# Two attention problems on one core: a longer list of fixed-point heads, four P buffers, earlier terms at a unit's end, a warmed TensorE and a shorter tail

## Chip, cores, metric

The kernel runs on one core of a Trainium2 chip. The metric is device time in microseconds, a median over runs.

## The reference

Two attention blocks read different inputs of 2048 rows, 512 columns, 32 heads of 16, and write side by side.

```python
# A: causal attention inside 4 segments of 512 rows, plus a memory of the earlier segments
for s in range(4):
    p = softmax(qs @ ks.T * 0.25 + causal_mask)
    o = g * (phi(qs) @ M) / (phi(qs) @ z + 1e-6) + (1 - g) * (p @ vs)
    M, z = M + phi(ks).T @ vs, z + phi(ks).sum()
# B: full softmax attention over 2048 keys
o = softmax(q @ k.T * 0.25) @ v
out = concat([oA @ A_wo, oB @ B_wo])
```

B dominates: 32 heads x 2048 queries x 2048 keys of exponentials.

## The kernel before

The kernel cuts the work into *units*: 512 queries and four heads, 32 units of A and 32 of B. A B unit has 64 *banks* of scores (16 key blocks x 4 heads, each 128x512 in one PSUM bank). Two engines make the exponential. ScalarE takes tiles of three or two banks, writes bf16 into a P buffer. VectorE makes it in fixed point: it adds a constant to the scaled score, stores int16 into a pD buffer, and reads the bits as f16; two further copies, offset by constants ("terms"), are each multiplied by its own scaled copy of V, and the three sum to a good exponential. So a bank on VectorE costs an *eviction* from PSUM, two cheap additions, and three value matmuls instead of one.

The order of all instructions is decided when the program is built: a Python loop keeps a clock for each engine and issues what its rules allow. TensorE executes in that order.

```python
PDB, PTB, XB = 3, 3, 5                     # pD, P and input buffers
E1 = [(13, 0), (14, 1), (15, 2)]           # second heads for VectorE: (key block, head)
u["dl"] = [(kb, kb % 4, kb) for kb in range(NSB)] + [(kb, j, NSB + n) for n, (kb, j) in enumerate(E1)]
                                           # 16 + 3 = 19 banks of a B unit meant for VectorE
def pick(u, n, but=None):                  # the banks of ScalarE's next tile
    if not nbanks(u):                      # ScalarE's own are gone: it takes VectorE's leftovers
        ...
def dve_adds():                            # the two further terms of a finished pair of banks
    ...
# [cut] in the loop:
if (pd_open["add"] is not None or pd_open["tile"] is not None) and du is None and c["dve"] + 300 <= t:
    dve_close(); continue                  # terms of an open pair: when VectorE has been idle
if (rd and (even >= 3 or done or ...) and (act_soon is None or act_soon > t + 200)):
    flush(u, 16 if done else min(even, 4) if even >= 3 else 3); continue    # value matmuls
```

```python
def setup_gates():                         # emitted before the first scores
    nc.scalar.activation(gcol[:], beta_t[:], ACT.Exp, scale=-1.0)   # waits for beta's DMA
    # [cut] VectorE: gcol, omg, mqg; GpSimd: maskg
    init_v(VP_b, NSB)                      # GpSimd memsets
    for m in mbds:
        nc.gpsimd.memset(m[:], 0.0)
```

The tail runs twelve output matmuls ahead of the last unit's last value matmuls, then that unit's finish, four output matmuls, four casts, and a check of the range of all 1024 columns of row sums, whose result (a flag) decides whether a slow general path must run.

## Time and profile before

| | before |
|---|---|
| median | 974.75 us |
| span of the profiled run | 976.6 us |
| busy: ScalarE, VectorE | 864.9, 753.5 us |
| evictions by VectorE / banks of B by ScalarE | 534 / 1514 |
| first exponential | 17.01 us |
| ScalarE's gaps from the first to the last exponential | 79.3 us |
| end of the last exponential to the end | 19.76 us |

The last three rows are counted from the timeline. An engine's busy time is a union; its gaps are what is left of a stretch.

From the page: the span, the busy times, and three groups. A group line holds line, engine, operation, output and input, shapes and count, then total busy us, mean ns of one, then idle us ahead of them and who ended it.

```profile
span 976.6 us, 18041 instructions
...
PE 822.3 (84%) x6974; PEld 255.7 (26%) x6974; DVE 753.5 (77%) x1502; ACT 864.9 (89%) x803; POOL 373.0 (38%) x768
...
L734 ACT ACTIVATE pT<-s_ps 128x1536 bf16<-128x1536 f32 (+2 forms) x613 | 701.5, 1253 | 68.8 <-PE d_ps L775 38.0
L786 DVE TENSOR_SCALAR pD<-d_ps 128x512 int16<-128x512 f32 x534 | 350.1, 680 | 56.6 <-PE d_ps L775 54.4
...
L752 DVE TENSOR_SCALAR pD<-pD 128x1024 int16<-128x1024 int16 (+1 forms) x538 | 234.1, 477 | 0.3
...
```

A bank costs ScalarE 701.5/1514 = 0.463 us and VectorE (350.1 + 234.1)/534 = 1.09 us. ScalarE is nearest to full.

What ended ScalarE's waits from 100 to 950 us (us in total, times, longest us):

```profile
...
ACT pT L734 <- PE d_ps L775: 38.0, 48, 3.3
ACT pT L734 <- PE s_ps L729: 23.4, 30, 6.8
...
```

The first line reads: ScalarE's next scores stood in TensorE's order behind a score matmul for VectorE (d_ps).

The start on the timeline (start, duration, engine and line, operation; in brackets the idle time before and what ended it), first ScalarE:

```profile
...
17.01 2.15 ACT L677 ACTIVATE pT<-s_ps 128x1280 bf16<-128x1280 f32 x2 [0.49 <-PE s_ps L667]
21.50 2.15 ACT L677 ACTIVATE pT<-s_ps 128x1280 bf16<-128x1280 f32 x2 [2.35 <-PE s_ps L667]
...
26.78 2.15 ACT L677 ACTIVATE pT<-s_ps 128x1024 bf16<-128x1024 f32 x2 [2.63 <-PE s_ps L667]
```

and GpSimd:

```profile
...
19.32 0.21 POOL L167 TENSOR_TENSOR maskg<-jm,mq 128x16 f32<-128x16 f32 x1 [15.26 <-issue]
...
21.66 1.44 POOL L134 MEMSET VP_b<- 128x64 bf16 x16
...
23.27 1.84 POOL L173 MEMSET mbd<- 128x1024 bf16 x2
25.07 3.22 POOL L688 TENSOR_SCALAR_AFFINE_SELECT pT<-pT 128x384 bf16<-128x384 bf16 x7
```

and TensorE:

```profile
...
17.89 3.25 PE L327 MATMUL d_ps<-wv_a,xT_a 128*128 128x512 bf16 x8
...
25.65 0.76 PE L877 MATMUL acc<-pT,VP_a 128*32 128x512 bf16 x5 [2.58 <-POOL pT L688]
...
```

GpSimd's gate masks and memsets ran from 19.3 to 25.1 us. The causal masks of the first units (L688) waited for them, TensorE's value matmuls waited 2.58 us for a mask, and the scores behind them came late: ScalarE stood idle for 2.63 us. Its 2.35 us of idle time before that had another cause: eight matmuls of a V projection (L327) stood ahead of the scores in TensorE's order until 21.1 us.

The tail on the timeline:

```profile
...
956.44 2.75 PE L494 MATMUL s_ps<-wo_b,OT 128*128 128x512 bf16 x12 [0.54 <-ACT pT L734]
...
964.67 0.67 DVE L1088 TENSOR_SCALAR g<-RA 128x1024 f32<-128x1024 f32 x1
...
966.05 1.23 DVE L1092 TENSOR_TENSOR g<-g,g 128x1024 f32<-128x1024 f32 x1
...
967.31 1.22 DVE L1101 TENSOR_REDUCE okc<-g 128x1 f32<-128x1024 f32 x1
...
969.47 0.15 DVE L1105 CAST flag<-okc 128x1 int32<-128x1 f32 x1 [0.55 <-POOL okc L1104]
```

The range check is the three middle lines shown, 964.67 to 968.53 us, with one more cut; the line at 969.47 us writes the flag.

### The profile page before, as it was taken

What the parts mean: (1) busy time and instruction counts of PE and PEld (TensorE: products, weight loads), DVE (VectorE), ACT (ScalarE), POOL (GpSimd) and SP (SyncE); (2) the same over time, 40 slices, a digit from 0 to 9 for tenths busy, and PEclk for the clock granted to TensorE, in tenths of its full rate; (3) what the DMA queues carried; (4) which work ended last, traced back from release to release, by engine and by line L of the source; (5) the groups of instructions that cost most, each with busy time, mean ns of one, the idle gap of its engine ahead of it and who ended that gap; (6) DMA issues with size and microseconds to landing.
All of it is one profiled execution on the core that took longest, in us unless ns stands there. A gap on an engine that the chain in (4) does not pass through costs nothing.

```text
span 976.6 us, 18041 instructions
## 1 busy us (share of the span) xinstructions
PE 822.3 (84%) x6974; PEld 255.7 (26%) x6974; DVE 753.5 (77%) x1502; ACT 864.9 (89%) x803; POOL 373.0 (38%) x768
## 2 busy tenths in 40 slices
PE   5999998888888888898888898788988878888784
PEld 2333232222222222232222222222322222222221
DVE  3454668787888788869888987987478987989774
ACT  3898979898998889899999998989999998989982
POOL 3850625233333443444443154326345421514320
PEclk9999999898998999899999999999989998989977
DMA  7011000000000000010000000000000000000001
GB/s 221 23 44 39 6 22 2 1 1 2 1 2 12 12 1 1 6 34 1 1 1 18 6 1 1 1 1 3 22 1 12 12 1 2 1 1 1 1 7 42
DMA packets 14719, 13.83 MB, mean 14 GB/s; under 512 B 2336, under 2 KB 14624, under 8 KB 14624
## 3 DMA queue, kind: packets, MB, share of 16 engines
q1 hardware_dynamic: 12864, 11.54, 3.7%
q8 instruction: 56, 0.92, 0.4%
q10 hardware_dynamic: 1632, 1.05, 0.4%
q14 instruction: 39, 0.32, 0.1%
q0 software_dynamic: 128, 0.00, 0.0%
HBM read 8.39 MB, written 4.19 MB: 13 GB/s over the span
## 4 chain that ended last, share of the span: by engine, by line
PE 32%; ACT 28%; DVE 16%; issue 14%; POOL 9%; DMA 1%; ACTq 0%; DVEq 0%; POOLq 0%
ACT pT L734 23%; PE acc L877 13%; PE s_ps L729 8%; DVE pD L786 7%; DVE pD L752 5%; ACT pT L677 4%; POOL VD L612 4%; PE d_ps L324 3%; POOL pT L688 2%; PE d_ps L327 2%; DVE tT L815 2%; PE d_ps L494 2%; PE d_ps L775 1%; PE s_ps L667 1%; DMA beta_t<-in_A_beta_dram 1%
## 5 line engine op out<-in xcount | busy, mean ns | idle before, releaser
L734 ACT ACTIVATE pT<-s_ps 128x1536 bf16<-128x1536 f32 (+2 forms) x613 | 701.5, 1253 | 68.8 <-PE d_ps L775 38.0
L786 DVE TENSOR_SCALAR pD<-d_ps 128x512 int16<-128x512 f32 x534 | 350.1, 680 | 56.6 <-PE d_ps L775 54.4
L729 PE MATMUL s_ps<-QT_b,KT_b 32*128 32x512 bf16 x1514 | 242.1, 398 | 70.2 <-ACT pT L734 62.9
L877 PE MATMUL acc<-pT,VP_b 128*32 128x512 bf16 x1514 | 268.1, 409 | 0.0
L877 PE MATMUL acc<-pD,VD 128*32 128x512 f16 x1602 | 240.5, 409 | 4.2 <-DVE tT L815 4.0
L752 DVE TENSOR_SCALAR pD<-pD 128x1024 int16<-128x1024 int16 (+1 forms) x538 | 234.1, 477 | 0.3
L688 POOL TENSOR_SCALAR_AFFINE_SELECT pT<-pT 128x512 bf16<-128x512 bf16 (+3 forms) x192 | 97.7, 525 | 288.2 <-ACT pT L677 287.9
L775 PE MATMUL d_ps<-QT_b,KT_b 32*128 32x512 bf16 x534 | 186.4, 396 | 15.1 <-DVE pD L786 13.0
L729 PEld LDWEIGHTS <-KT_b 32*128 32x128 bf16 x1514 | 70.2, 91 | 295.3 <-issue 288.9
L677 ACT ACTIVATE pT<-s_ps 128x1024 bf16<-128x1024 f32 (+1 forms) x128 | 136.7, 1169 | 10.9 <-PE s_ps L667 9.4
L877 PEld LDWEIGHTS <-VP_b 128*32 128x32 bf16 x1514 | 68.5, 98 | 76.0 <-issue 54.4
L877 PEld LDWEIGHTS <-VD 128*32 128x32 bf16 x1602 | 59.5, 98 | 96.0 <-issue 83.1
L667 PE MATMUL s_ps<-QT_a,KT_a 32*128 32x384 bf16 (+3 forms) x512 | 57.7, 303 | 24.2 <-ACT pT L677 12.2
L612 POOL TENSOR_SCALAR VD<-VP_b 128x288 bf16<-128x288 bf16 (+1 forms) x186 | 66.9, 360 | 12.2
L815 DVE STREAM_TRANSPOSE tT<-acc 128x512 f32<-128x512 f32 x64 | 45.5, 711 | 31.4 <-PE acc L877 30.7
L877 PE MATMUL acc<-pT,VP_a 128*32 128x384 bf16 (+3 forms) x512 | 49.0, 318 | 16.2 <-POOL pT L688 12.8
L836 POOL TENSOR_TENSOR tN<-tT,RA 128x256 bf16<-128x256 f32 x31 | 20.1, 650 | 77.5 <-DVE RA L818 77.4
L337 POOL TENSOR_SCALAR QT_b<-qc,mq 128x512 bf16<-128x512 bf16 x32 | 24.1, 763 | 66.2 <-DVE qc L395 66.0
L775 PEld LDWEIGHTS <-KT_b 32*128 32x128 bf16 x534 | 40.1, 91 | 9.0 <-issue 7.7
L667 PEld LDWEIGHTS <-KT_a 32*128 32x128 bf16 x512 | 20.4, 92 | 79.5 <-issue 69.2
L337 POOL TENSOR_SCALAR QT_a<-qc,mq 128x512 bf16<-128x512 bf16 x30 | 21.8, 736 | 35.6 <-DVE qc L393 35.4
L504 DVE CAST osb<-d_ps 128x512 bf16<-128x512 f32 x28 | 19.1, 685 | 12.7 <-PE d_ps L494 12.7
(109 smaller groups left out, 613.9 us busy)
## 6 DMA issues: line engine op xcount, KB each, us to landing
out_dram<-osb SPq DMA_DIRECT2D x30, 128.0 KB, 1.7
xin<-in_B_x_dram SPq DMA_DIRECT2D x16, 128.0 KB, 2.2
xin<-in_A_x_dram SPq DMA_DIRECT2D x14, 128.0 KB, 2.1
wv_a<-in_A_wv_dram SPq DMA_DIRECT2D x1, 512.0 KB, 10.4
wv_b<-in_B_wqkv_dram SPq DMA_DIRECT2D x1, 512.0 KB, 9.9
wk_b<-in_B_wqkv_dram SPq DMA_DIRECT2D x1, 512.0 KB, 9.6
wq_b<-in_B_wqkv_dram SPq DMA_DIRECT2D x1, 512.0 KB, 10.0
wo_a<-in_A_wo_dram SPq DMA_DIRECT2D x1, 512.0 KB, 9.4
```

Of the source, the lines that this page charges most:

```text
L337: nc.gpsimd.tensor_scalar(t[:, par, :], qc[:], mq[:, par:par + 1], 1.0, ALU.mult, ALU.mult)
L612: mul = lambda dst, src: nc.gpsimd.tensor_scalar(dst, src, EXP_C[k], 1.0, ALU.mult, ALU.mult)
L667: nc.tensor.matmul(pt[:, b, col:col + w], kt[32 * j:32 * j + 32, kbl * P:(kbl + 1) * P], q[32 * j:32 * j + 32, P * kbl:512], start=(r == 0 ...
L677: nc.scalar.activation(pT[:].rearrange("p b n -> p (b n)")[:, 0:n], pt[:].rearrange("p b n -> p (b n)")[:, 0:n], ACT.Exp, scale=0.25)
L688: nc.gpsimd.affine_select(out=blk, in_=blk, compare_op=ALU.is_ge, fill=0.0, base=0, pattern=[[0, e - b], [0, w // P], [1, P]], channel_mul ...
L729: nc.tensor.matmul(pt[:, b, :], KT_b[32 * j:32 * j + 32, u["rt"], kb * P:(kb + 1) * P], q[32 * j:32 * j + 32, :], start=True, stop=True, t ...
L734: nc.scalar.activation(pT[:, 0:n, :], pt[:, 0:n, :], ACT.Exp, scale=1.0 / (LOG2E * 1024.0))
L752: nc.vector.tensor_scalar(tile[:, k, 0:n, :], tile[:, 0, 0:n, :], EXP_D[k], None, ALU.add)
L775: nc.tensor.matmul(bank[:], KT_b[32 * j:32 * j + 32, u["rt"], kb * P:(kb + 1) * P], qslice(u)[32 * j:32 * j + 32, :], start=True, stop=Tru ...
L786: nc.vector.tensor_scalar(pd[:, 0, n, :], bank[:], EXP_B, 0.0, ALU.add, ALU.max)
L815: nc.vector.transpose(tT[:].rearrange("p c d -> p (c d)"), u["acc"][:])
L877: nc.tensor.matmul(u["acc"][32 * j:32 * j + 32, e["c0"]:512], e["lhsT"], e["rhs"], start=(j not in u["started"]), stop=False, tile_positio ...
```

## The change

The intent: give VectorE more banks, let the plan balance the two engines as it goes, end units earlier, and shorten both ends. A *flush* is a batch of value matmuls; *chores* are the projections and output matmuls that TensorE fits in between; *fill* matmuls of zeros keep TensorE busy. Cut to its core:

```diff
-    PDB, PTB, XB = 3, 3, 5
+    PDB, PTB, XB = 3, 4, 5          # paid for by 3 instead of 4 Q and K tiles
-    E1 = [(13, 0), (14, 1), (15, 2)]
+    E1 = [(9, 0), (10, 1), (11, 2), (13, 0), (14, 1), (15, 2)]
 def pick(u, n, but=None):
+        while nbanks(u) and len(u["dl"]) > 1 and len(u["dl"]) * 1050 > nbanks(u) * 470 + LEAD:   # LEAD = 1000
+            kb, j, _ = u["dl"].pop()
+            u["al"][j].append(kb)     # the "rule": hand a bank back to ScalarE
+        dve_end(u)
+    def dve_end(u):                   # called after every eviction, too
+        if not u["dl"] and (pd_open["tile"] is not None or pd_open["add"] is not None):
+            dve_close()               # terms of the unit's last bank(s) at once
     # flushes, chores and VectorE's banks sized to the time before ScalarE's next tile
-        if (rd and (even >= 3 or done or ...) and (act_soon is None or act_soon > t + 200)):
+        room = max(c["act"] - LATE, act_soon or 0) - t + SLK        # LATE, SLK = 470, 400
+        r = int(min(want, 4 if not done else 16, (room - DR) // MM))   # two even rounds are enough
     # start
+    warm_up(5) ... warm_up(6)         # matmuls of zeros before the first projections
-    setup_gates()
+    at(t0 + 9000, setup_gates)        # 9 us later on the plan's clock
     # tail
-        tail_open() as soon as ScalarE has no more tiles
+        tail_open() just ahead of the last finalize
-    range_of(nc.vector, 0, 64, g1, g2)
+    range_of(nc.gpsimd, 0, 62) earlier; range_of(nc.vector, 62, 64) at the end
     # [cut] latency constants of the plan, A's units spread a little earlier, more fill matmuls
```

## The prediction

> **What bounds the kernel now.** ScalarE. The page gives it 864.9 us busy of a 976.6 us span, VectorE 753.5. In the chain of waits the exponentials of B alone (L734) hold 23%. The windows view gives, from 100 to 950 us, ScalarE 92% busy, VectorE 82%. Of ScalarE's 112 us without work, counted from the timeline, 17 lie after its last exponential, 66 between 100 and 956 us (38.0 put down to score matmuls of VectorE's banks, L775, ahead of its own in TensorE's order), 11 between 16 and 100 us, the rest before its first one at 17.0 us.
>
> **What moves.** By the groups of instructions a bank (128x512) costs ScalarE 701.5/1514 = 0.463 us and VectorE (350.1+234.1)/534 = 1.09 us, and on VectorE's side TensorE two more value matmuls. The old plan gave VectorE 19 banks per B unit, but 534/31 = 17.2 were made; ScalarE took the rest at the units' ends. The new list has 22; the new rule in the pick cuts it to 20 when a unit starts and further where VectorE lags. I expect about 19.3, near 597 evictions and 1450 ScalarE banks: ScalarE -29 us (to about 836), VectorE +66 (to about 820). Nearly all of it is critical on ScalarE; VectorE has 154 us of gaps from 100 to 956 us to take it, but comes near 90% there, so the two then limit together and some gain returns as waits.
>
> **Start.** First score matmul at 16.57 us. The projections ran from 9.38 to 12.9 us at about 430 ns per matmul (timeline). The Trainium skill, "TensorE: Matmul & The Clock Gate", section "What's actually happening", says that an idle array runs at half clock and about 3.4 us of activity release it; this trace agrees (about 215 ns later). Eleven warm-up matmuls should halve the projections (-1.7 us). The gates' exponential waited for beta until 14.3 us and held VectorE's Q masks until 15.15; deferred, it no longer does (-2 us or more). GpSimd's memsets of VP_b held the first causal masks until 25.07 us and ScalarE idled 7.6 us around them; most of that goes. Together about -7 us.
>
> **Tail.** The twelve output matmuls ahead of the last value matmuls (2.75 us on the chain) run behind them; two leftover casts (1.25 us) go; the 1024-wide range check (3.9 us) becomes one of 32 columns (about 1 us), and the all-reduce runs beside the last casts. About -6 us; the 7 us after the flag's copy stay.
>
> **Middle.** Four P buffers, terms made at once, flushes sized to the time left before ScalarE's next tile: fewer scores wait behind value matmuls. ScalarE's gaps 66 -> perhaps 64, as a fuller VectorE eats most of it. Flushes of two rounds change array tiling more often; TensorE has room.
>
> **Sum.** 974.8 - 29 - 7 - 6 - 2 = about 931 us. Range 914 to 952. Faster by over 2%: 0.91; within: 0.08; slower: 0.01.
>
> **What would show it.** L734 busy falls to about 672 us; evictions (L786) 580 to 615; first exponential before 13 us; last exponential to end 14 us against 20; VectorE about 87% of the span, ScalarE still 89 to 90%; ScalarE's idle behind L775 below 30 us; projections at about 215 ns per matmul.
>
> **What would make it wrong.** If VectorE saturates, its banks hold ScalarE's scores in TensorE's order: gain under 25 us. If three QT/KT buffers instead of four make Q projections late, gaps open where units change. If ScalarE's idle shrinks more than I think (buffers, new flush rule), under 915. If the rule returns more banks, evictions stay near 540 and only start, tail and waits gain (about 955).

## The result

| | before | changed |
|---|---|---|
| median | 974.75 us | 960.81 us |
| ratio of fast runs | | 0.9866 (95%: 0.9842 to 0.9890) |
| span of the profiled run | 976.6 | 961.9 us |
| busy: ScalarE, VectorE | 864.9, 753.5 | 859.0, 780.0 us |
| evictions / ScalarE's banks of B | 534 / 1514 | 557 / 1491 |
| first exponential | 17.01 | 13.82 us |
| ScalarE's gaps, first to last exponential | 79.3 | 80.1 us |
| last exponential to end | 19.76 | 13.08 us |

A ratio is the mean time of one kernel's fast runs over that of the other's in the same rounds, so not quite the ratio of the medians quoted.

The gain is 1.3%, where 4.5% was forecast, and outside the range. The page of the changed kernel (L741 is the old L734, L793 the old L786):

```profile
span 961.9 us, 18348 instructions
...
PE 854.3 (89%) x7114; PEld 257.0 (27%) x7114; DVE 780.0 (81%) x1560; ACT 859.0 (89%) x796; POOL 382.4 (40%) x772
...
L741 ACT ACTIVATE pT<-s_ps 128x1536 bf16<-128x1536 f32 (+1 forms) x606 | 693.2, 1238 | 65.2 <-PE s_ps L736 32.0
L793 DVE TENSOR_SCALAR pD<-d_ps 128x512 int16<-128x512 f32 x557 | 363.3, 676 | 46.3 <-PE d_ps L782 41.4
...
```

Only 23 evictions were added, where 63 were expected. VectorE is far from saturated (81% of the span).

ScalarE's waits from 100 to 950 us:

```profile
...
ACT pT L741 <- PE s_ps L736: 31.3, 49, 1.7
ACT pT L741 <- PE d_ps L782: 27.2, 40, 3.4
...
```

The waits behind VectorE's score matmuls fell from 38.0 to 27.2 us, and those for its own score matmuls rose from 23.4 to 31.3 us.

The start, ScalarE, then GpSimd, then TensorE:

```profile
...
13.82 2.15 ACT L677 ACTIVATE pT<-s_ps 128x1280 bf16<-128x1280 f32 x2 [1.05 <-PE s_ps L667]
...
35.66 0.60 ACT L674 ACTIVATE pT<-s_ps 128x512 bf16<-128x512 f32 x1 [5.25 <-PE s_ps L667]
```

```profile
...
26.47 0.21 POOL L167 TENSOR_TENSOR maskg<-jm,mq 128x16 f32<-128x16 f32 x1
...
28.81 1.44 POOL L134 MEMSET VP_b<- 128x64 bf16 x16
...
30.42 1.83 POOL L173 MEMSET mbd<- 128x1024 bf16 x2
32.22 0.87 POOL L688 TENSOR_SCALAR_AFFINE_SELECT pT<-pT 128x512 bf16<-128x512 bf16 x2
...
```

```profile
...
32.90 0.62 PE L892 MATMUL acc<-pT,VP_a 128*32 128x128 bf16 x3 [3.61 <-POOL pT L688]
...
```

The GpSimd work did not go away: it moved from 19.3 to 26.5 us, into the stream of causal masks. TensorE's value matmuls waited 3.61 us for a mask, and ScalarE idled 5.25 us in one piece. The windows view shows what followed (per stretch: length, then busy us and count of PE, weight loads, DVE, ACT, POOL, then the granted clock):

```profile
...
core 0: us, PE busy (x) PEld busy (x) DVE busy (x) ACT busy (x) POOL busy (x), PEclk, DMA share, GB/s
30.00:35.00 5.00, 1.10 (x7) 0.34 (x6) 0.00 (x0) 0.41 (x1) 4.91 (x13) 0.70 0.00 0
35.00:40.00 5.00, 5.00 (x39) 2.42 (x36) 2.80 (x5) 2.86 (x3) 4.78 (x10) 0.50 0.35 105
40.00:45.00 5.00, 5.00 (x38) 1.56 (x36) 2.35 (x4) 3.30 (x4) 3.45 (x7) 0.78 0.00 0
...
```

In the first of these stretches TensorE and ScalarE almost stop; in the second the clock is at half. By 30 us ScalarE had finished 27 banks against 14 before; by 50 us it was 50 against 52, and by 100 us 152 against 152 (counted from the timeline). The whole lead of the start was gone.

The tail:

```profile
...
949.65 3.63 PE L494 MATMUL s_ps<-wo_b,OT 128*128 128x512 bf16 x16
...
952.13 0.19 DVE L1144 TENSOR_REDUCE okc<-g 128x1 f32<-128x32 f32 x1
...
952.83 0.38 POOL L1147 PARTITION_ALL_REDUCE okc<-okc  x1 [16.61 <-DVE okc L1146]
...
955.12 0.14 DVE L1153 CAST flag<-okc 128x1 int32<-128x1 f32 x1
...
```

The output matmuls run beside the finish, the check is 32 columns wide, and the all-reduce no longer follows the casts.

### The profile page after: what moved, and what is told of

It is laid out like the page before. It is cut to its first block, busy times and chain, and to the rows that moved or that the text cites. A ratio compares the mean times of both kernels' runs of the same rounds, so it can differ in the third digit from the quotient of the medians.

```text
span 961.9 us, 18348 instructions
## 1 busy us (share of the span) xinstructions
PE 854.3 (89%) x7114; PEld 257.0 (27%) x7114; DVE 780.0 (81%) x1560; ACT 859.0 (89%) x796; POOL 382.4 (40%) x772
## 4 chain that ended last, share of the span: by engine, by line
PE 42%; ACT 22%; DVE 16%; issue 9%; POOL 9%; DMA 1%; SPq 0%; ACTq 0%; DVEq 0%
ACT pT L741 19%; PE acc L892 16%; PE s_ps L736 9%; DVE pD L793 6%; DVE pD L759 5%; PE d_ps L324 4%; PE d_ps L782 3%; PE d_ps L327 3%; POOL VD L612 3%; POOL pT L688 3%; ACT pT L677 2%; DVE tT L828 2%; PE s_ps L667 2%; PE d_ps L494 2%; DMA wv_a<-in_A_wv_dram 1%
## 5 line engine op out<-in xcount | busy, mean ns | idle before, releaser
L741 ACT ACTIVATE pT<-s_ps 128x1536 bf16<-128x1536 f32 (+1 forms) x606 | 693.2, 1238 | 65.2 <-PE s_ps L736 32.0
L793 DVE TENSOR_SCALAR pD<-d_ps 128x512 int16<-128x512 f32 x557 | 363.3, 676 | 46.3 <-PE d_ps L782 41.4
L736 PE MATMUL s_ps<-QT_b,KT_b 32*128 32x512 bf16 x1491 | 251.7, 405 | 35.9 <-ACT pT L741 27.2
L892 PE MATMUL acc<-pT,VP_b 128*32 128x512 bf16 x1491 | 255.5, 399 | 0.1
L759 DVE TENSOR_SCALAR pD<-pD 128x1024 int16<-128x1024 int16 (+1 forms) x572 | 250.4, 481 | 0.5
L782 PE MATMUL d_ps<-QT_b,KT_b 32*128 32x512 bf16 x557 | 196.6, 397 | 23.4 <-DVE pD L793 17.6
L892 PEld LDWEIGHTS <-VP_b 128*32 128x32 bf16 x1491 | 61.0, 97 | 63.3 <-issue 46.6
L612 POOL TENSOR_SCALAR VD<-VP_b 128x288 bf16<-128x288 bf16 (+1 forms) x186 | 71.8, 386 | 12.3
L667 PE MATMUL s_ps<-QT_a,KT_a 32*128 32x512 bf16 (+3 forms) x512 | 59.1, 304 | 11.6 <-ACT pT L677 8.7
L892 PE MATMUL acc<-pT,VP_a 128*32 128x512 bf16 (+3 forms) x512 | 49.6, 342 | 14.8 <-POOL pT L688 14.5
L504 DVE CAST osb<-d_ps 128x512 bf16<-128x512 f32 x28 | 19.2, 684 | 18.7 <-PE d_ps L494 18.7
```

Of the source, the lines that this page charges most:

```text
L612: mul = lambda dst, src: nc.gpsimd.tensor_scalar(dst, src, EXP_C[k], 1.0, ALU.mult, ALU.mult)
L667: nc.tensor.matmul(pt[:, b, col:col + w], kt[32 * j:32 * j + 32, kbl * P:(kbl + 1) * P], q[32 * j:32 * j + 32, P * kbl:512], start=(r == 0 ...
L736: nc.tensor.matmul(pt[:, b, :], KT_b[32 * j:32 * j + 32, u["rt"], kb * P:(kb + 1) * P], q[32 * j:32 * j + 32, :], start=True, stop=True, t ...
L741: nc.scalar.activation(pT[:, 0:n, :], pt[:, 0:n, :], ACT.Exp, scale=1.0 / (LOG2E * 1024.0))
L759: nc.vector.tensor_scalar(tile[:, k, 0:n, :], tile[:, 0, 0:n, :], EXP_D[k], None, ALU.add)
L782: nc.tensor.matmul(bank[:], KT_b[32 * j:32 * j + 32, u["rt"], kb * P:(kb + 1) * P], qslice(u)[32 * j:32 * j + 32, :], start=True, stop=Tru ...
```

## The experiments

A profile is one execution. The changed kernel was run in three sessions in all (the result, e6 and e16; e6 and e16 on different chips): medians 960.81, 960.41 and 959.25 us, but ScalarE's gaps in the three profiles were 80.1, 70.7 and 69.5 us. So single-profile gaps carry some 10 us of chance; banks, busy times and durations repeat. Times of one kernel spread by 5 us either way; below, ratios to the kernel before in the same rounds decide, with their 95% intervals. The count of banks is fixed when a program is built, so it was known before each run. Only e5, e7 and e8 (beside e6) and e13 to e15 (beside e16) had the changed kernel in the same rounds; elsewhere it is compared across sessions.

A run's time also goes with its mean granted clock: in the rounds of e1 the kernel before took 968.81 us at 0.957 and 979.48 us at 0.942. No experiment holds the clock fixed, so it is a rival that stays untested wherever two kernels were granted different clocks.

Theory A, the prediction's: the list and the rule set VectorE's share, and the moved banks carry the gain. Theory B: the list does not bind; VectorE's share is set by when a bank can be placed, and other parts carry the gain.

### e1_three_extra

```diff
 # changed kernel
-    E1 = [(9, 0), (10, 1), (11, 2), (13, 0), (14, 1), (15, 2)]
+    E1 = [(13, 0), (14, 1), (15, 2)]     # and the matching scaling of V
```

> The changed kernel with the second list of VectorE's heads cut back from six to three (19 banks per B unit at most, as before); everything else stays. The program's own count is 551 evictions against 557. Theory A (the longer list is what moves banks, as I predicted): evictions fall back and the time rises by 3 us or more, to 964 to 970 us. Theory B (VectorE's share is set by how often a bank can be placed: pD buffers, chores due, the planner's order, and the list is never what binds in an ordinary unit): within 3 us of the changed kernel, 958 to 964 us.

Measured: 963.86 us, ratio 0.9899 (0.9852 to 0.9946), 551 evictions. The three extra heads account for 6 of the 23 added banks. The time lies between the two theories; the count decides for B.

### e2_no_rule

```diff
-        while nbanks(u) and len(u["dl"]) > 1 and ...
+        while False and nbanks(u) and len(u["dl"]) > 1 and ...
```

> The changed kernel with the new rule in the pick switched off, so that all 22 banks stay VectorE's until ScalarE has none left and takes the rest, as before the change. The program holds 552 evictions against 557. Theory A (the rule hands banks back that VectorE could have made; named in the prediction as what could make it wrong): more evictions and a shorter time, by 5 us or more. Theory B (VectorE cannot be given more whatever the list says): no more evictions, time within 3 us of the changed kernel.

Measured: 952.82 us, ratio 0.9772 (0.9726 to 0.9819), 552 evictions. Neither theory had it: no more banks move, as B says, yet its ratio is below those of the changed kernel (0.9831 to 0.9866 in three sessions, none in these rounds; the interval overlaps that of e6). The rule handed back 118 banks in the plan; without it ScalarE takes 130 at the units' ends instead. Whether the second is better, and why, is not settled.

### e3_three_p_buffers

```diff
-    PDB, PTB, XB = 3, 4, 5
+    PDB, PTB, XB = 3, 3, 5
```

> The changed kernel with three P buffers per slot instead of four; the program holds 553 evictions, flushes go from 469 to 523. Theory B says that the fourth P buffer, not the moved banks, carries what the middle gained: ScalarE then waits for value matmuls to free P, its gaps between first and last exponential grow from 80 us to 90 us or more, and the time goes to 968 to 978 us. Theory A (moved banks carry the gain) expects less than 3 us more, since the number of banks hardly changes.

Measured: 963.48 us, ratio 0.9896 (0.9840 to 0.9952). By the ratios 0.3 to 0.65% are lost against the changed kernel, within the intervals; ScalarE's gaps were 74.1 us, not the 90 expected. The plan's own clock had said 15 us (917.3 against 902.1): that clock is no measure of this.

### e4_memsets_first

```diff
     gcol = const.tile([P, HG], F32, name="gcol")
+    init_v(VP_b, NSB)
+    for m in mbds:
+        nc.gpsimd.memset(m[:], 0.0)
     # removed from setup_gates; its maskg part becomes setup_masks
     at(t0 + 9000, setup_gates)
+    at(t0 + 60000, setup_masks)
```

> The changed kernel with GpSimd's memsets of VP_b and of the memory matrices back at the very start (GpSimd idles there from 4 to 19 us) and the memory masks made 60 us in; ScalarE's and VectorE's part of the gates stays where the change put it. Theory: the 5.25 us gap of ScalarE at 30.4 to 35.7 us and the half clock from 33 to 42 us come from 5.8 us of GpSimd work that the change moved from 19 to 26 us, into the stream of causal masks. Then the gap goes, the clock stays full, 60 or more instead of 50 ScalarE banks are done by 50 us, and the time falls by 4 to 8 us to about 955. Rival: the first units are bounded by the masks themselves and the lead is lost elsewhere; then less than 2 us.

Measured: 952.45 us, ratio 0.9783 (0.9737 to 0.9830); against the changed kernel's three ratios 5 to 8 us. GpSimd's part of the start, on the timeline:

```profile
...
4.03 1.47 POOL L134 MEMSET VP_b<- 128x64 bf16 x16
...
5.64 1.86 POOL L151 MEMSET mbd<- 128x1024 bf16 x2
```

and the windows that were broken in the changed kernel, same columns:

```profile
...
30.00:35.00 5.00, 5.00 (x58) 2.40 (x56) 3.52 (x8) 4.95 (x6) 4.92 (x11) 1.00 0.35 105
35.00:40.00 5.00, 4.95 (x41) 1.66 (x42) 2.71 (x5) 4.70 (x6) 4.92 (x11) 1.00 0.01 3
...
```

The clock is 1.00, ScalarE is full, 64 banks are done by 50 us (50 in the changed kernel) and 167 by 100 us (152). The theory holds: the deferred gates cost what the start had won. The trace shows the mechanism; the size is loose, since the interval overlaps that of e6.

### e6_changed_again

No edit: the changed kernel as reference beside e5, e7 and e8.

> The changed kernel once more, unaltered, as the reference on the chip and in the rounds of the three kernels that run beside it. Expected: 958 to 964 us, ratio to the kernel before 0.984 to 0.989.

Measured: 960.41 us, ratio 0.9831 (0.9796 to 0.9867).

### e5_two_pd_buffers

```diff
-    PDB, PTB, XB = 3, 4, 5
+    PDB, PTB, XB = 2, 4, 5
```

> The changed kernel with two pD buffers instead of three. The program holds 496 evictions instead of 557, so 61 banks go back to ScalarE; list and rule stay. It asks whether the pD buffers are what sets VectorE's share, and what a moved bank is worth. If my price of 0.463 us per bank on ScalarE is all critical: 28 us slower than the changed kernel, about 989 us. If ScalarE's banks are only partly critical (its gaps take some of it): less than 14 us slower.

Measured: 978.50 us, ratio 1.0047 (1.0009 to 1.0085). The exponentials' group of e6, then that group and the evictions of e5:

```profile
...
L741 ACT ACTIVATE pT<-s_ps 128x1536 bf16<-128x1536 f32 (+1 forms) x606 | 692.7, 1236 | 58.6 <-PE d_ps L782 29.2
...
```

```profile
...
L741 ACT ACTIVATE pT<-s_ps 128x1536 bf16<-128x1536 f32 (+1 forms) x634 | 720.9, 1243 | 48.2 <-PE s_ps L736 25.7
L793 DVE TENSOR_SCALAR pD<-d_ps 128x512 int16<-128x512 f32 x496 | 326.5, 679 | 91.8 <-PE d_ps L782 90.1
...
```

The exponentials of B grow by 28.2 us, exactly 61 banks at 0.462; the medians differ by 18.1 us. So list and rule unchanged, one buffer less takes 61 banks away: the pD buffers limit VectorE's share, and about two thirds of ScalarE's added work reaches the time. (The mean granted clock was 0.960 in e5's runs and 0.942 in e6's, so this is not a bank's price alone.)

### e7_memsets_no_rule

Both edits, e2 and e4, together.

> Memsets first and no rule together; 552 evictions. If the two gains seen (0.8% from the memsets, 0.9% for no rule, against another chip's run of the changed kernel) are real and independent: ratio to the changed kernel beside it 0.983 to 0.986, about 945 us. If the gain without the rule was the chip's difference: 0.990 to 0.993, about 952 us.

Measured: 950.31 us, ratio 0.9728 (0.9683 to 0.9773), 0.990 of e6. This is what was written for "the gain without the rule was the chip's difference"; the medians say the same. The rule's cost is therefore shown less firmly than the memsets'.

### e8_four_pd_buffers

```diff
 # on top of e7
-    PDB, PTB, XB = 3, 4, 5
+    PDB, PTB, XB = 4, 4, 4           # and one tN and one tM buffer less
-    LATE, SLK, EVEN = 470.0, 400.0, 2
+    LATE, SLK, EVEN = 470.0, 800.0, 2
```

> Memsets first, no rule, and in addition four pD buffers (paid for with one input, one tN and one tM buffer) and the slack of the flush rule at 800 ns instead of 400. The program holds 580 evictions instead of 552. If a bank moved to VectorE is worth its 0.463 us on ScalarE: 13 us faster than memsets-and-no-rule beside it. If VectorE is near its limit or its banks stand in front of ScalarE's scores: under 4 us.

Measured: 944.22 us, ratio 0.9676 (0.9644 to 0.9708), the best version of all. The exponentials' group of e7 (L744 is L741), then that group and the evictions of e8:

```profile
...
L744 ACT ACTIVATE pT<-s_ps 128x1536 bf16<-128x1536 f32 (+2 forms) x614 | 696.0, 1234 | 58.7 <-PE s_ps L739 29.5
...
```

```profile
...
L744 ACT ACTIVATE pT<-s_ps 128x1536 bf16<-128x1536 f32 (+1 forms) x603 | 682.6, 1230 | 58.6 <-PE d_ps L785 26.5
L796 DVE TENSOR_SCALAR pD<-d_ps 128x512 int16<-128x512 f32 x580 | 374.4, 673 | 23.2 <-PE d_ps L785 21.0
...
```

28 banks take 13.4 us off the exponentials and the median falls by 6.1 us, about half. The expectation of "13 us if all is critical" fails by the medians; "under 4" is not excluded, since the two intervals overlap. A moved bank is worth roughly 0.2 us upward (e8, loosely) and 0.3 us downward (e5), not 0.463. The slack changed too, so the bank's own worth is not isolated.

### e9_tail_only

The changed kernel's tail (output matmuls beside the last finish, split range check) put alone into the kernel before.

```diff
+            if pvi[0] == len(U) - 1:
+                tail_open()
             finalize(u, pvi[0] == len(U) - 1)
-    range_of(nc.vector, 0, 64, g1, g2)
+    range_of(nc.gpsimd, 0, 62)  # earlier
+    range_of(nc.vector, 62, 64)
```

> The kernel before with the changed tail alone (last output matmuls beside the last unit's finish, range check of 62 slots on GpSimd ahead of the last unit); the program holds 533 evictions against 534. The tail of the changed kernel measured 13.1 us against 19.8. Expected if the tail's term of the prediction was right: 5 to 8 us faster than before, 967 to 970 us, with 13 to 14 us from the last exponential to the end. If the tail only hid behind something else: under 3 us.

Measured: 974.65 us, ratio 0.9971 (0.9935 to 1.0007). In the profile the last exponential ends 15.1 us before the end, against 19.8. The 4.6 us are within the interval, but so is nothing. The other 2 us of the changed tail need the rest of the change: it is 15.6 us in e13, which lacks only the closing.

### e10_list_only

```diff
 # kernel before
-    E1 = [(13, 0), (14, 1), (15, 2)]
+    E1 = [(9, 0), (10, 1), (11, 2), (13, 0), (14, 1), (15, 2)]
```

> The kernel before with the list of VectorE's second heads lengthened from three to six, alone. The program holds 540 evictions against 534. Theory A (the list sets the share): more banks move and it is faster by 5 us or more. Theory B (the list is not what binds): six banks more, within 3 us of the kernel before; perhaps slower, since GpSimd also scales six more value blocks.

Measured: 982.31 us, ratio 1.0074 (1.0042 to 1.0106), 540 evictions. Theory A is refuted: the longer list alone moves six banks and makes the kernel slower. In that plan ScalarE picks up 142 leftovers at the units' ends (55 before) and runs ten more tiles (623 against 613) for six banks fewer; that this is the cause was not tested. The rival named beforehand, GpSimd's scaling of six more value blocks (L612: 66.9 us before, 70.4 here), was not tested either.

### e11_old_flush

```diff
 # changed kernel
-            r = int(min(want, 4 if not done else 16, (room - DR) // MM)) ...
+        if (rd and (even >= 3 or done or ...) and (act_soon is None or act_soon > t + 200)):
+            flush(u, 16 if done else min(even, 4) if even >= 3 else 3)
-                    if room >= 4 * MM + DR:                # chores
+                    if act_soon is None or act_soon > t + 300:
-                elif du is not None and room >= MM + DR:   # VectorE's banks
+                elif du is not None and (act_soon is None or act_soon > t + 400):
```

> The changed kernel with the old conditions for flushes, chores and VectorE's banks (three rounds at least, fixed distances to ScalarE's next tile) in place of the sized ones; the program holds 543 evictions against 557 and 406 flushes against 469. If the sized flushes carry what the middle gained: 4 to 10 us slower than the changed kernel, 965 to 970 us, with more ScalarE gaps. If not: only the 14 banks' worth, 3 to 5 us (at 0.22 to 0.34 us a bank).

Measured: 954.41 us, ratio 0.9778 (0.9733 to 0.9823). A miss of both: with 14 banks fewer it is not slower but, if anything, faster. The sized flushes carry no gain.

### e12_no_warm_up

```diff
-    warm_up(5)
-    warm_up(6)
```

> The changed kernel without its eleven warm-up matmuls; the same plan, 557 evictions. Expected from the prediction: the eight projection matmuls take about 430 ns each again and the first exponential comes 1.7 us later. Since the GpSimd work in the mask stream stops the early units anyway, I expect no difference in the whole: within 2 us of the changed kernel.

Measured: 958.53 us, ratio 0.9811 (0.9780 to 0.9842): no loss. The first four projection matmuls of e12, and then of the changed kernel with the first V projection, on TensorE's timeline:

```profile
...
9.18 1.89 PE L324 MATMUL s_ps<-xT_a,wq_a 128*128 128x512 bf16 x4 [2.45 <-DMA wq_a<-in_A_wq_dram]
...
```

```profile
...
9.46 1.04 PE L324 MATMUL s_ps<-xT_a,wq_a 128*128 128x512 bf16 x4 [1.84 <-DMA wq_a<-in_A_wq_dram]
...
12.43 1.02 PE L327 MATMUL d_ps<-wv_a,xT_a 128*128 128x512 bf16 x4 [1.07 <-DMA wv_a<-in_A_wv_dram]
...
```

The warm-up does what it should: 1.89 us become 1.04. It buys no time: the first V projection of the changed kernel still waited for the weights' DMA, and the first exponential came at 14.74 us in e12, and at 13.82, 15.04 and 16.79 us in the changed kernel's three profiles.

After these runs it was open what carried the gain at all: 23 banks at 0.2 to 0.3 us are 5 to 7 us, and the start carried nothing.

### e13_no_end_close

```diff
     def dve_end(u):
-        if not u["dl"] and (pd_open["tile"] is not None or pd_open["add"] is not None):
-            dve_close()
+        return
```

> The changed kernel without the closing of VectorE's open pair at a unit's end (its terms then come when VectorE has been idle for a while, as before); 550 evictions against 557. If the earlier terms shorten the units' ends: slower by 4 us or more than the changed kernel beside it, more waits of the unit's first transposition for its value matmuls. If not: within 3 us.

Measured: 973.09 us, ratio 0.9953 (0.9902 to 1.0003), beside 0.9833 for the changed kernel on the same chip: 12 us, most of the gain. The exponentials' group on the page of e13:

```profile
...
L741 ACT ACTIVATE pT<-s_ps 128x1536 bf16<-128x1536 f32 (+2 forms) x611 | 697.2, 1240 | 70.0 <-PE s_ps L736 37.8
...
```

L741's idle time is 70.0 us here; it is 65.2, 58.6 and 56.1 us in the changed kernel's three profiles, so the first of them is barely apart. Over all profiles it is clearer: from 100 us to the last exponential, counted from the timelines, ScalarE's gaps are 68.4 to 75.2 us in the four without the closing (before, e9, e10, e13) and 51.8 to 67.8 us in the sixteen with it (of which all but e17 and e18 carry the rest of the change as well). Where in a unit the gaps shrink is less clear: from 4 us before to 3 us after a unit's first transposition (VectorE's first step in finishing a unit; units after 100 us, overlaps counted once) ScalarE's idle time is 37.1 us in e13, and 34.0, 33.0 and 29.6 us in the changed kernel, but 40.9 and 39.2 us in e8 and e14, which close too. The expected sign, more waits of that transposition (L827) for its value matmuls, did not show: from 100 to 950 us 16.2 us, against 21.9 in e16. Seven banks fewer account for some 2 us. The clock is a rival here: its mean was 0.927 in e13's runs and 0.944 in e16's.

### e14_old_flush_p3

```diff
 # on top of e11
-    PDB, PTB, XB = 3, 4, 5
+    PDB, PTB, XB = 3, 3, 5
-    at(t0 + 9000, setup_gates)
+    at(t0 + 5000, setup_gates)     # at 9000 the first unit would read the gates before they are made
```

> The changed kernel with the old conditions for flushes, chores and VectorE's banks and three P buffers (the gates 5 us in instead of 9, since the first finish comes earlier in this plan); 542 evictions against 543 with the old conditions and four P buffers. If the fourth P buffer matters under the old conditions: 8 us or more slower than those conditions with four (954 us, ratio 0.978), about 963 us or more. If it never matters: within 3 us of them.

Measured: 962.84 us, ratio 0.9875 (0.9829 to 0.9921), 1% above e11, on another chip. The fourth P buffer is worth some 8 or 9 us under the old conditions by the medians, with intervals that just fail to meet; the earlier gates were changed along with it.

### e15_all_and_old_flush

e8 with the old condition for flushes (three rounds at least) and the new ones for chores and VectorE's banks.

> Memsets first, no rule, four pD buffers, slack 800 ns, and the old condition for flushes (three rounds at least), the new ones for chores and VectorE's banks; 577 evictions and 354 flushes, against 580 and 420 in the best version so far (944 us, ratio 0.968). If fewer, larger flushes help there too: ratio 0.960 to 0.965. If not: 0.966 to 0.971.

Measured: 954.89 us, ratio 0.9782 (0.9736 to 0.9828). A miss: the old flush, harmless in e11, seems to cost 1% here against e8 (0.9676, on another chip).

### e16_changed_third

No edit: the reference beside e13 to e15.

> The changed kernel, unaltered, as the reference beside the three others: ratio to the kernel before 0.982 to 0.988.

Measured: 959.25 us, ratio 0.9833 (0.9787 to 0.9878).

### e17_end_close_only

The function dve_end and its calls, put alone into the kernel before.

```diff
+    def dve_end(u):
+        if not u["dl"] and (pd_open["tile"] is not None or pd_open["add"] is not None):
+            dve_close()
     # called at the end of dve_bank, and where pick takes the leftovers
```

> The kernel before with the closing of VectorE's open pair at a unit's end, alone; 527 evictions against 534, so no bank moves to VectorE (7 fewer). If the earlier unit ends carry the middle of the change: 6 to 12 us faster than before, 963 to 969 us, in spite of the 7 banks. If they need the rest of the change: within 3 us of the kernel before.

Measured: 968.90 us, ratio 0.9920 (0.9897 to 0.9943): 7.8 us of the mean, though 7 banks went the wrong way. The exponentials' group on the page of e17 (L735 is L734):

```profile
...
L735 ACT ACTIVATE pT<-s_ps 128x1536 bf16<-128x1536 f32 (+2 forms) x615 | 704.7, 1258 | 60.5 <-PE d_ps L776 30.8
...
```

L734's idle falls from 68.8 us to 60.5 us while its work grows from 701.5 to 704.7 us; around the units' ends, counted as for e13, it falls from 39.2 to 32.7 us. No bank explains this, nor does the clock: its mean was 0.941 in e17's runs and 0.946 in the kernel before beside it.

### e18_end_close_four_p

```diff
 # on top of e17
-    PDB, PTB, XB = 3, 3, 5
+    PDB, PTB, XB = 3, 4, 5     # and 3 Q and K tiles, as in the change
```

> The same with four P buffers and three Q and K buffers; 540 evictions. If the fourth P buffer adds (the plan's own clock says 14 us): 5 us or more faster than the closing alone. If not, as undoing it in the changed kernel suggested: within 3 us of the closing alone.

Measured: 965.43 us, ratio 0.9884 (0.9854 to 0.9915), 540 evictions. Four P buffers add some 3.5 us; the intervals overlap. The plan's own clock had promised 14.

## Why the prediction was wrong

**ScalarE bounds the kernel: right.** e5 gave it 28.2 us more work and the time rose by 18.1 us. The Trainium skill, "Perfetto Trace Analysis", section "Identifying the Most-Contended Engine", says to optimize the engine of highest occupancy first; this case agrees (ScalarE 864.9 us, VectorE 753.5), but the exchange rate is below one. In the changed kernel TensorE's 854.3 us of busy time come close to ScalarE's 859.0; whether it had become a second limit was not tested.

**"I expect about 19.3, near 597 evictions ... ScalarE -29 us": wrong, and this is the step that failed.** The program moved 23 banks, not 63; at 0.463 us that is 10.6 us of ScalarE, and ScalarE's busy time fell by 5.9 us on the page. I divided 534 by 31 units and read the average of 17.2 as a plan that fell short everywhere. The program's own counts say otherwise: four units made 9, 13, 8 and 4 banks (the first two after B's start, and the two just ahead of A's third and fourth segment), and these four hold 42 of the 55 missing banks; the other 27 units made 16 to 19 (the first unit of B has no list). Counted the same way in the changed program, the four such units make 52 banks instead of 34 and the other 27 make 505 instead of 500: 18 of the 23 new banks came from the four, and an ordinary unit went from 18.5 to 18.7 banks. Neither the list (e1, e10) nor the rule (e2) set that share. The pD buffers do for the most part: with two, three and four of them the 27 units make 444, 505 and 521 banks, in all 496, 557 and 580 (e5, e6, e8, the last with more slack); the conditions for placing a bank move 14 more (e11, 543). The prediction had named an outcome near the measured one, "evictions stay near 540 ... (about 955)", but for a wrong reason: it blamed the rule, and without it the program makes 552.

**"Nearly all of it is critical on ScalarE": too high as well.** A bank's 0.463 us were worth about 0.3 us when taken (e5) and about 0.2 us when given (e8); the rest turned into gaps. Even 63 banks would have brought 13 to 19 us, not 29.

**Start, "together about -7 us": wrong in the sum.** The first exponential did come 3.2 us earlier in that profile (0.2 to 3.2 in the three), but the prediction treated GpSimd's 5.8 us as gone, where the diff only moved them, and it put down to GpSimd 2.35 us of idle time that a V projection had caused. GpSimd's work fell into the mask stream, stopped ScalarE for 5.25 us, and the lead was zero by 100 us. e4 removes the cause and gains 5 to 8 us by the ratios.

**Warm-up: mechanism right, worth nothing.** The projections halved, as forecast, and e12 loses nothing without it.

**Tail, "about -6 us": right in the profile** (19.76 to 13.08 us). Alone it shortens the tail by 4.6 us, and its effect on the time is not resolved (e9).

**Middle, "-2 us": much too small.** I listed "terms made at once" in one clause and gave it no number. Alone it brings 7.8 us (e17), and taking it out of the change costs 12 us (e13). The gaps of all profiles agree; where in a unit they shrink is not settled, and in e13 the clock differed too. The likely path is that a unit's last terms hold back its last value matmuls, and with them the single accumulator that the next unit needs; this path was argued, and the waits that should show it did not. Four P buffers add some 3.5 us (e18), the sized flushes nothing by themselves (e11).

The parts do not add up like independent terms: the same flush condition is harmless in e11 and seems to cost 1% in e15. The sizes come near the gain of 13 us: closing and P buffers 11 us (ratio 0.9884 in e18, with six more banks), a tail 6.7 us shorter in the profile, a start that gives nothing, and a longer list that by itself costs 7 us (e10). But this sum is no test: taking the list's three heads out of the changed kernel (e1) won nothing back.

**Overlooked: TensorE's granted clock.** In the changed kernel's windows view ScalarE all but stops where the clock is halved:

```profile
...
192.00:196.00 4.00, 4.00 (x32) 0.98 (x31) 2.38 (x6) 1.45 (x2) 0.00 (x0) 0.57 0.02 4
196.00:200.00 4.00, 3.57 (x38) 1.08 (x31) 4.00 (x10) 4.00 (x5) 0.00 (x0) 1.00 0.00 0
...
```

Counted from the trace between 100 and 950 us, the kernel before spent 99.0 us at half clock, and 36.2 of ScalarE's 68.4 us of idle time fell into them; the changed kernel spent 112.6 us, with 36.3 of 67.8 us. Half of the gaps that every theory above argues about lie there. Whether the slow clock makes ScalarE wait, or the same waits leave TensorE idle and so slow its clock, no run here shows.

**Open:** why the kernel without the rule is not slower (its mean clock was 0.954, the changed kernel's 0.939 to 0.944), whether the leftovers on ScalarE are what makes e10 slower, and how much of e8's gain is banks and how much slack.

## What to carry to other kernels

A count that is fixed when the program is built should be counted, not estimated: the changed program gave VectorE 557 banks, not 597, before it ever ran. Nor is it enough to look at how many units reach the end of a list: 18 of the 31 did before, and the longer list alone still moved only six banks. Build it with that one change and count. When work is deferred, ask what it will stand in front of at its new place, above all on an in-order engine that others wait for. Small rules at the end of a unit of work, where a single accumulator passes from one to the next, deserve a number of their own in the sum.

## What the Trainium skill lacked or had wrong

- "TensorE: Matmul & The Clock Gate", section "Why this matters for your kernels", advises no idle gap of TensorE over about 3 us between bursts. The changed kernel agrees: after a wait of 3.61 us (on the timeline, ended by a causal mask at 32.90 us) the granted clock was 0.50 from 35 to 40 us and 0.78 to 45 us. But the rule in that section was not enough here: between 100 and 950 us of the same trace the clock fell to half 21 times, and no gap of TensorE there was longer than 1.81 us.
- "Perfetto Trace Analysis", section "Identifying the Most-Contended Engine", gives no exchange rate between work taken off the fullest engine and time: here 18.1 us of time for 28.2 us of work (e5), and 6.1 us for 13.4 us (e8).
